# Attention with a routed feed-forward: the row transposes move into the accumulator's banks, value products follow their scores by 3 to 6 steps, and the first expert's rows are prepared earlier

## The chip, the core and the metric

The kernel runs on one core of a Trainium2 chip, in one launch. The core has a matrix engine (PE, whose weight loads are shown apart as PEld), a vector engine (DVE), a scalar engine (ACT), a general engine (POOL) and SyncE (SP), which here only issues transfers. DMA queues move data between memory and the on-chip buffers. Each engine runs its own instructions in order and waits on semaphores for the others. Matrix products land in accumulator banks; in this kernel a bank is a tile of 128 partitions by 512 fp32 numbers. The metric is the time of one execution in microseconds; lower is better.

## The reference

Attention over 8 batches, 12 heads, 448 positions and 64 columns a head, with soft-capped scores, and then a feed-forward whose expert is chosen per token, by a gate with a bias per modality:

```python
scores = scale * np.matmul(q, k.transpose(0, 1, 3, 2))
scores = cap * np.tanh(scores / cap)
scores = scores - np.max(scores, axis=-1, keepdims=True)
attn = np.exp(scores)
attn = attn / (np.sum(attn, axis=-1, keepdims=True) + 1e-09)
return np.matmul(attn, v).astype(np.float32)
...
logits = x @ w_gate + modality_bias[modality_id]
e_idx = np.argmax(logits, axis=1)
...
    h = np.maximum(x[mask] @ w1[e], 0.0)
    out[mask] = gate_w[mask, None] * (h @ w2[e])
```

Here `x` is the attention's result, 3584 tokens of 768 columns. There are 8 experts with 768 x 1024 and 1024 x 768 weights.

## The kernel before

**Attention.** Four heads make a group; there are 24 groups `d` (three to a batch), and each has 7 steps `s` of 64 keys. Step `n = 7d + s` is, in this order: the scores of 64 keys against all queries of four heads (`scores`, L445, into one of two `sc` tiles of two banks each), a tanh over them on ACT (L449), and after every second step one exp over both steps (L452). `weigh` multiplies the weights with the values (L467) into the accumulator `xT`, which is one tile of two banks, and follows the scores by `LAG` = 4 steps; its place is shifted around s = 4 and 5 (no value products at s = 4, two at s = 5). DVE adds the weights up over the steps (L473 and L475, `tot`) and copies the accumulator out after the seventh (L478, `kept`). `pin` keeps an instruction in the order in which the program was written, on its engine.

**Rows.** At s = 4 of group d four things follow the scores on PE. `logits(d - 2)` turns the sums and gate products of an earlier group (L496), and DVE takes reciprocals and scales them (L499, L505). `go_on` gives the pending routing its next piece (L240 and L242 on PE are its rank). `tokens(d - 2)` transposes the four heads' result into token rows (L520), which DVE scales (L527, one instruction) and a DMA stores to `xd` (L534). `sums(d - 1)` multiplies sums and gate weights (L485, L487), copied out at L489. The tile `tp` of `tokens` is taken from the pool of `sc` (tag "sc", two tiles in turn), so transposes and scores share four banks.

**Routing.** `start_route` after a batch's third group picks each token's expert in small DVE pieces and scatters token numbers and weights into a map in memory by four indirect DMAs (L266, tile `pay`, one buffer). `gate_bias` loads modality numbers and bias table and builds the bias with five DVE instructions (L195, L196, L203); the loads are issued on SP at the start of group 1.

**The way to the feed-forward.** The last batch's tokens are routed late, and work begins with one tile of 384 tokens of an expert that has as many among the first seven batches. SOON = 20 is the last group of the seventh batch. Its routing runs at (d, s) = (21, 6) and (22, 2), where `early_slot` also counts the tokens (L281 on PE) and DVE picks the expert (`emeta`, L301). At (22, 4) come the token rows of group 20, stored by SP, and the load of the map (`mt`, L677), which waits for the scatters. At (23, 1) POOL gathers the 384 rows (`xg`, L686, three indirect DMAs). The first expert's w1 comes in six blocks, each split into a high part (cast, L704) and the rest (L705): blocks 0, 1 and 2 on POOL at (22, 6) and (23, 1), block 3 on DVE at (23, 5), blocks 4 and 5 cast on ACT and subtracted on DVE after the loop. Then `move` transposes the gathered rows on PE (L722), split by ACT (L731) and DVE (L732), among the last value products.

**Feed-forward.** Slots of 384 tokens: `ffn1` (L749, L750, L753, tile `ph`, three buffers) and `ffn2` (L778). In the first slot the remaining sums, logits, routing and slot table of the last batch are put between the `ph` products. This part takes the time from about 375 us on.

**Start.** Six products of ones (`warm`, L160) run while the cap is loaded; the flag read follows, then four more, then the scores.

The line that shares the banks, and the two that set the lag:

```python
tp = ps_s.tile([128, 2, 512], F32, name="tp", tag="sc")
...
for m in range(n - LAG - (s == 5), n - LAG + (s != 4)):
    if m >= 0:
        weigh(m)
```

## Time and profile before

| | us |
|---|---|
| median of three runs (902.51 to 909.3) | 905.6 |
| the profiled execution | 906.49 |
| its span, from the first instruction to the last | 904.9 |
| first scores on PE start | 7.94 |
| last tanh of the attention starts | 357.15 |
| first product of the feed-forward starts | 375.04 |
| busy: PE, ACT, DVE, POOL | 850.4, 531.8, 515.4, 157.1 |

Busy time on PE is modelled at the ends of products, so a product's own duration overlaps the next; what PE needs for a piece of work is read from start to start. A row of a timeline gives the start, the duration, the engine, the line, what is written from what, and in brackets how long the engine was idle before and whom it waited for. PE counts each fp32 product as two instructions, so a step's four score products show as x8.

### The profile page before, as it was taken

Reading aid. Unit: us, or ns where it says so; the run is one execution under the profiler, and the core shown is the slowest. Engines: PE = TensorE matmul, PEld = TensorE weight load, DVE = VectorE, ACT = ScalarE, POOL = GpSimd, SP = SyncE. Lnnn points to the kernel's source line nnn. Section 1 sums busy time; section 2 is a strip of 40 time slices with the busy share of each in tenths; the row PEclk is TensorE's granted clock in tenths of the full one; section 3 lists DMA queues with packets and bytes.
Section 4 is the critical chain, followed back from the end, with each engine's and each line's share of the span. In section 5 each row is a group of like instructions: output and inputs, shape, how many; then the busy total and the mean of one; then the engine's idle time right before and its main releaser. Section 6 shows DMA issues by size and latency. Waiting matters only on the chain. (4 is left out here: it accounts for less than half of the span.)

```text
span 904.9 us, 15828 instructions
## 1 busy us (share of the span) xinstructions
PE 850.4 (94%) x6208; PEld 637.5 (70%) x6208; DVE 515.4 (57%) x867; ACT 531.8 (59%) x624; POOL 157.1 (17%) x161
## 2 busy tenths in 40 slices
PE   7799999999999998698999999999999999999996
PEld 2233334333343333598999999999999999989896
DVE  2568777778686877665443443444343344447861
ACT  6698898988989888315443442444433343436551
POOL 2000302031211214725202020120203011021000
PEclk9899999999999999699999999999999999999998
DMA  4235444363644456518735355464535446447650
GB/s 134 89 122 164 102 143 121 126 158 99 154 106 140 109 140 205 166 42 266 257 109 193 114 168 193 151 234 134 200 121 167 147 156 211 135 141 230 212 188 6
DMA packets 44284, 136.92 MB, mean 151 GB/s; under 512 B 8526, under 2 KB 9102, under 8 KB 44192
## 3 DMA queue, kind: packets, MB, share of 16 engines
q1 hardware_dynamic: 35008, 103.10, 36.6%
q0 software_dynamic: 9040, 32.64, 11.5%
q8 instruction: 52, 0.85, 0.4%
q14 instruction: 40, 0.33, 0.1%
q10 hardware_dynamic: 144, 0.00, 0.0%
HBM read 114.20 MB, written 22.69 MB: 151 GB/s over the span
## 5 line engine op out<-in xcount | busy, mean ns | idle before, releaser
L449 ACT ACTIVATE pt<-sc,isc 128x896 f32<-128x896 f32 x168 | 162.7, 996 | 46.7 <-PE sc L445 45.5
L753 PE MATMUL ph<-x,al 128*128 128x384 f32 (+2 forms) x528 | 168.2, 319 | 0.0
L778 PE MATMUL py<-bh,hh 128*128 128x384 f32 x464 | 158.5, 342 | 1.2 <-ACT hh L759 1.2
L778 PE MATMUL py<-bh,hl 128*128 128x384 f32 x464 | 155.8, 336 | 0.0
L778 PE MATMUL py<-bl,hh 128*128 128x384 f32 x464 | 155.3, 335 | 0.0
L467 PE MATMUL xT<-pt,va 64*64 64x448 f32 x1344 | 153.7, 542 | 0.0
L452 ACT ACTIVATE pt<-pt,cabs 128x1792 f32<-128x1792 f32 x84 | 150.3, 1789 | 2.7
L475 DVE TENSOR_TENSOR tot<-tot,pt 128x896 f32<-128x896 f32 x120 | 133.1, 1109 | 23.7 <-ACT pt L452 19.0
L749 PE MATMUL ph<-x,ah 128*128 128x384 f32 x384 | 130.3, 339 | 4.5 <-DVE x L732 4.4
L750 PE MATMUL ph<-x,ah 128*128 128x384 f32 x384 | 129.7, 338 | 0.0
L705 DVE TENSOR_TENSOR bl<-raw,bh 128x768 fp32r<-128x768 f32 x84 | 77.7, 955 | 50.0 <-ACT bh L704 49.9
L467 PEld LDWEIGHTS xT<-pt,va 64*64 64x64 f32 x1344 | 51.8, 135 | 76.4 <-issue 76.3
L704 ACT CAST bh<-raw 128x768 fp32r<-128x768 f32 x88 | 70.2, 839 | 57.0 <-DMA raw<-in_w_dram 52.7
L753 PEld LDWEIGHTS ph<-x,al 128*128 128x128 f32 x528 | 102.3, 194 | 0.0
L788 POOL DMA_INDIRECT out_dram<-ot,mt x29 | 32.0, 1105 | 385.8 <-ACT ot L783 308.4
L759 ACT ACTIVATE hh<-ph 128x384 fp32r<-128x384 f32 x64 | 30.6, 488 | 108.1 <-PE ph L753 105.2
L445 PE MATMUL sc<-kq 64*64 64x448 f32 x672 | 83.0, 569 | 9.8 <-ACT pt L449 9.0
L783 ACT ACTIVATE ot<-py,mt 128x384 f32<-128x384 f32 x58 | 33.7, 581 | 95.6 <-PE py L778 52.6
L778 PEld LDWEIGHTS py<-bh,hh 128*128 128x128 f32 x464 | 87.1, 188 | 1.6 <-ACT hh L759 1.5
L778 PEld LDWEIGHTS py<-bl,hh 128*128 128x128 f32 x464 | 87.2, 188 | 0.2 <-DVE bl L705 0.2
L778 PEld LDWEIGHTS py<-bh,hl 128*128 128x128 f32 x464 | 87.1, 188 | 0.1
L760 DVE SCALAR_TENSOR_TENSOR hl<-ph,hh 128x384 fp32r<-128x384 f32 x64 | 34.9, 555 | 91.7 <-ACT hh L759 91.5
(157 smaller groups left out, 1053.3 us busy)
## 6 DMA issues: line engine op xcount, KB each, us to landing
raw<-in_w_dram SPq DMA_DIRECT2D x88, 384.0 KB, 4.9
raw<-in_w_dram SPq DMA_DIRECT2D x64, 512.0 KB, 4.8
kq<-in_kq_dram SPq DMA_DIRECT2D x24, 448.0 KB, 5.0
va<-in_v_dram SPq DMA_DIRECT2D x24, 448.0 KB, 6.0
kx<-in_kq_dram SPq DMA_DIRECT2D x24, 448.0 KB, 4.4
xd<-xs POOLq DMA_DIRECT2D x23, 448.0 KB, 4.0
kq<-in_w_dram SPq DMA_DIRECT2D x2, 512.0 KB, 6.5
mapd<-pay,pos POOLq DMA_INDIRECT x32, 8.2
```

The costliest lines, as they stand in the source:

```text
L445: pin(pe.matmul(sc[i * KB : (i + 1) * KB, j, :S], kq[rows, s * KB : (s + 1) * KB], kq[rows, S:QK], start=True, stop=True,))
L449: pin(nc.scalar.activation(weights(n), sc[:, :, :S], AF.Tanh, scale=self.isc))
L452: pin(nc.scalar.activation(pt, pt, AF.Exp, scale=self.cabs))
L467: pin(pe.matmul(self.xT[j * D : (j + 1) * D, i, :S], vas[d][rows, o : o + D], pt[rows, j], start=s == 0, stop=s == STEPS - 1,))
L475: pin(V.tensor_tensor(tots[d], tots[d], pt, op=ALU.add))
L704: keep((cast.tensor_copy if cast else self.nc.scalar.copy)(hi, raw))
L705: keep((minus or self.nc.vector).tensor_tensor(lo, raw, hi, op=ALU.subtract))
L749: nc.tensor.matmul(ph[:, :w], hi[:, fs], self.x[:, k, 0, :w], start=first, stop=False)
L750: nc.tensor.matmul(ph[:, :w], hi[:, fs], self.x[:, k, 1, :w], start=False, stop=False)
L753: nc.tensor.matmul(ph[:, :w], lo[:, fs], self.x[:, k, 0, :w], start=False, stop=last)
L760: nc.vector.scalar_tensor_tensor(hl[:, f, :w], acc, 0.0, hh[:, f, :w], op0=ALU.max, op1=ALU.subtract)
L778: nc.tensor.matmul(py[:, :HALF], self.h[a][:, f, rows], self.w2s[f][c][:, cs], start=i == 0, stop=i == 3 * FC - 1,)
```

## The change

Value products get a table: `LAGS` gives for each step how many steps later it is weighed, 5, 5, 5, 5, 4, 4, 3 in even groups and 6, 5, 5, 5, 4, 4, 3 in odd ones, and `LAST` for the last group. With it no value products stand at s = 3 and 4, and the accumulator is copied out at s = 2 of the next group. The transposes of `tokens` take the accumulator's tile (tag "xT" of `ps_x`), at s = 4; the scaling is two DVE instructions, one for each bank. `sums` moves to s = 5, after that step's scores. `logits` is split: `turn` transposes and takes the reciprocals ahead of `tokens`, the scaling of the logits follows it. The additions leave `weigh` and run four steps behind the scores (`add`, `BEHIND`). The modality loads are issued at step 0 and used at (1, 3). Ahead of the first scores 18 products of ones run in one piece instead of six and four.

Near the end: the piece of routing and `early_slot` move from (22, 2) to (22, 1); the rows of group 20 from (22, 4) to (22, 2), into two banks of other pools and with their store ahead of the map's load on SP; the map's load to (22, 2); the gather from (23, 1) to (22, 4); all w1 loads to (22, 2), with blocks 4 and 5 in tiles of their own; the splits 0, 1, 2 and 3 to (22, 2), (22, 4), (22, 4) and (23, 4). Four `move`s instead of three stand ahead of the last two value products, in the banks of `sc`. The last group's remaining four additions and its copy come after all moves. `pay` has two buffers.

```diff
-LAG = 4
+LAGS = ((5, 5, 5, 5, 4, 4, 3), (6, 5, 5, 5, 4, 4, 3))
+LAST = (6, 5, 4, 4, 4, 4, 4)
+BEHIND = 4
...
+    def fetch_bias(self):
...
+        pay = pool.tile([CP, C, 2], F32, name="pay" if tok is not None else f"pay{b % 2}")
...
+            def add(n):
+
+                d, s = divmod(n, STEPS)
+                if s == 1:
+                    tots[d] = xp.tile([128, 2, S], F32, name="tot", bufs=2)
+                if s:
+                    pin(V.tensor_tensor(tots[d], pt_of(n - 1) if s == 1 else tots[d], pt_of(n), op=ALU.add))
...
-                if s == 1:
-                    tots[d] = xp.tile([128, 2, S], F32, name="tot", bufs=2)
-                    pin(V.tensor_tensor(tots[d], pt_of(n - 1), pt, op=ALU.add))
-                elif s:
-                    pin(V.tensor_tensor(tots[d], tots[d], pt, op=ALU.add))
-                if s == STEPS - 1:
-                    kept[d] = xp.tile([128, 2, S], F32, name="xT", bufs=3)
-                    pin(V.tensor_copy(kept[d], self.xT[:, :, :S]))
+
+            def keep(d):
+                kept[d] = xp.tile([128, 2, S], F32, name="xT", bufs=3)
...
-            def logits(d):
+            def turn(d):
...
+
+            def logits(d):
+
...
-                    tp = ps_s.tile([128, 2, 512], F32, name="tp", tag="sc")
+                    tp = ps_x.tile([128, 2, 512], F32, name="tp", tag="xT")
...
-                if not banks:
-                    src = tp[:CP].rearrange("p i (c j d) -> p i c j d", c=C, j=2)
-                    pin(V.tensor_tensor(dst, src, norm, op=ALU.mult))
...
+                for i in range(2):
+                    src = tps[i][:CP].rearrange("p (c j d) -> p c j d", c=C, j=2)
+                    pin(V.tensor_tensor(dst[:, i], src, norm[:, i], op=ALU.mult))
...
-                    raws[k] = self.load_raw(self.first_e, self.w1, k, FF, firsts[k - 4] if k >= 4 else None)
+                    spare = xp.tile([128, FF], F32, name="spare", bufs=2) if k >= 4 else None
+                    raws[k] = self.load_raw(self.first_e, self.w1, k, FF, spare)
...
-            self.warm(self.ps_r, 4)
+            END = STEPS * ND
+            due = [[] for _ in range(END + 1)]
+            for m in range(END):
+                d, s = divmod(m, STEPS)
+                due[min(m + (LAST if d == ND - 1 else LAGS[d % 2])[s], END)].append(m)
...
-                        self.gate_bias()
+                    if d == 0:
+                        self.fetch_bias()
...
                 scores(n)
-                if s == 6 or s == 1 and d != SOON + 2:
+                if n >= BEHIND:
+                    add(n - BEHIND)
+                if (d, s) == (1, 3):
...
-                if s == 4 and d:
-                    if d >= 2 and d - 2 != SOON:
+                if s == 4 and d >= 2:
+                    if d - 2 == SOON:
+                        self.gather(maps, known=NT - S)
+                    else:
+                        turn(d - 2)
+                        go_on()
+                        tokens(d - 2)
                         logits(d - 2)
-                    if d >= 2:
-                        go_on()
-                        tokens(d - 2, nc.sync if d - 2 == SOON else nc.gpsimd)
+                if s == 5 and d:
                     sums(d - 1)
-                    if d - 2 == SOON:
-                        maps = self.rows(meta, 0, early=True)
-                        load_w1((2, 3))
-                    elif d >= 2 and (d - 2) % NU == NU - 1:
+                    if d >= 2 and d - 2 != SOON and (d - 2) % NU == NU - 1:
                         start_route((d - 2) // NU)
-                for m in range(n - LAG - (s == 5), n - LAG + (s != 4)):
-                    if m >= 0:
-                        weigh(m)
+                for m in due[n]:
+                    weigh(m)
+                    if m % STEPS == STEPS - 1:
+                        keep(m // STEPS)
                 if (d, s) == (SOON + 1, 6):
+                    turn(SOON)
                     logits(SOON)
                     start_route(SOON // NU)
                     go_on()
                     go_on()
-                if (d, s) == (SOON + 2, 2):
+                if (d, s) == (SOON + 2, 1):
                     go_on()
                     meta = self.early_slot(self.cpool, self.ps_r)
                     self.first_e = self.expert(meta, 0)
                     load_w1((0, 1))
-                if (d, s) == (SOON + 2, 6):
+                if (d, s) == (SOON + 2, 2):
+                    tokens(SOON, nc.sync, (self.ps_r, "small"), (ps_g, "glog"))
+                    maps = self.rows(meta, 0, early=True)
+                    load_w1((2, 3, 4, 5))
                     split(0, nc.gpsimd, nc.gpsimd)
-                if (d, s) == (SOON + 3, 1):
-                    self.gather(maps, known=NT - S)
+                if (d, s) == (SOON + 2, 4):
                     split(1, nc.gpsimd, nc.gpsimd)
                     split(2, nc.gpsimd, nc.gpsimd)
-                if (d, s) == (SOON + 3, 5):
+                if (d, s) == (SOON + 3, 4):
                     split(3, V, V)
 
...
-            def move(k):
-                self.transpose(k, *((self.ps_r, "small") if k % 3 == 2 else (ps_s, "sc")), pin=True)
-
-            n = STEPS * ND
-            weigh(n - 4)
-            weigh(n - 3)
+            def move(k, pt):
+                self.transpose(k, None, None, pin=True, pt=pt)
+
+            for n in due[END][:2]:
+                weigh(n)
             split(4, None, V)
-            for k in range(3):
-                move(k)
-            weigh(n - 2)
-            weigh(n - 1)
+            pair = [ps_s.tile([128, 2, 512], F32, name="ptr", tag="sc") for _ in range(2)]
+            for k in range(4):
+                move(k, pair[k // 2][:, k % 2])
+            for n in due[END][2:]:
+                weigh(n)
             split(5, None, V)
-            for k in range(3, KC):
-                move(k)
+            move(4, self.ps_r.tile([128, 512], F32, name="ptr", tag="small"))
+            move(5, ps_g.tile([128, 512], F32, name="ptr", tag="glog"))
+            for n in range(END - BEHIND, END):
+                add(n)
...
+                turn(ND - 2)
...
+                turn(ND - 1)
...
-                    self.warm(ps_w, 6)
+                    self.warm(ps_w, 18)
```

On PE, the stretch of an even group around the transposes. `sc` are scores, `lt` the turned sums and logits, `tp` the token rows, `glog` the products of sums and gate, `xT` the value products. Before:

```order
L445 MATMUL sc<-kx 64x448 [waits Activation_49]
L445 MATMUL sc<-kx 64x448 x3
L496 MATMUL lt<-ident,gl 112x128 [waits DVE_49]
L496 MATMUL lt<-ident,gl 112x128 x3
L520 MATMUL tp<-ident,xT 112x128 [waits Activation_49]
L520 MATMUL tp<-ident,xT 112x128 x7
L485 MATMUL glog<-tot,pick 32x448 [waits DVE_49]
L485 MATMUL glog<-tot,pick 32x448
L487 MATMUL glog<-xT,wgt 32x448 [waits DVE_49]
L487 MATMUL glog<-xT,wgt 32x448
L445 MATMUL sc<-kx 64x448 [waits Activation_49]
L445 MATMUL sc<-kx 64x448 x3
```

And in the changed kernel, where these rows stand at the same place in another such group:

```order
L506 MATMUL lt<-ident,gl 112x128 [waits DVE_49]
L506 MATMUL lt<-ident,gl 112x128 x3
L534 MATMUL tp<-ident,xT 112x128 [waits DVE_49]
L534 MATMUL tp<-ident,xT 112x128 x7
L451 MATMUL sc<-kx 64x448 [waits Activation_49]
L451 MATMUL sc<-kx 64x448 x3
L495 MATMUL glog<-tot,pick 32x448 [waits DVE_49]
L495 MATMUL glog<-tot,pick 32x448
L497 MATMUL glog<-xT,wgt 32x448 x2
L451 MATMUL sc<-kx 64x448 [waits Activation_49]
L451 MATMUL sc<-kx 64x448 x3
L481 MATMUL xT<-pt,va 64x448 [waits DMAHW1_49,DVE_49,PE_49]
```

The transposes no longer wait for ACT but for DVE's copy of the accumulator, the next scores stand straight behind them, and the wait for DVE's reading of `tp` has moved from a later score to the next group's first value product.

On DVE at the start, groups 0 and 1 (`modi` and `mbt` are the modality numbers and the bias table). Before, the bias stands behind the second addition:

```order
L473 TENSOR_TENSOR tot<-pt 128x896 [waits Activation_49]
L475 TENSOR_TENSOR tot<-tot,pt 128x896 [waits DVE_49,Activation_49]
L195 TENSOR_SCALAR sel<-modi 112x32 [waits DMAHW3_49]
L196 TENSOR_TENSOR bias<-sel,mbt 112x256 [waits DMAHW4_49,DVE_49]
L195 TENSOR_SCALAR sel<-modi 112x32 [waits DVE_49]
```

Now it stands behind the first group's copy of the accumulator and its last addition:

```order
L469 TENSOR_TENSOR tot<-tot,pt 128x896 [waits DVE_49]
L488 COPY xT<-xT 128x896 [waits PE_49]
L469 TENSOR_TENSOR tot<-tot,pt 128x896 [waits DVE_49,Activation_49]
L201 TENSOR_SCALAR sel<-modi 112x32 [waits DMAHW0_49]
L202 TENSOR_TENSOR bias<-sel,mbt 112x256 [waits DMAHW1_49,DVE_49]
L201 TENSOR_SCALAR sel<-modi 112x32 [waits DVE_49]
```

All six of the first group's additions have moved ahead of the wait for `modi`.

On DVE behind the last scores (`al` is the rest of a w1 block, `x` the rest of the gathered rows, `hl` the first result of the feed-forward). Before:

```order
L705 TENSOR_TENSOR al_157<-kq,ah_156 128x1024 [waits DMAHW4_49,DMAHW0_49,Activation_49]
L732 TENSOR_TENSOR x<-ptr,x 128x384 [waits Activation_49] x3
L475 TENSOR_TENSOR tot<-tot,pt 128x896 [waits DVE_49] x2
L478 COPY xT<-xT 128x896 [waits PE_49]
L705 TENSOR_TENSOR al_159<-kq,ah_158 128x1024 [waits DMAHW5_49,DMAHW1_49,Activation_49]
L732 TENSOR_TENSOR x<-ptr,x 128x384 [waits Activation_49] x3
```

Now:

```order
L732 TENSOR_TENSOR al_169<-spare,ah_168 128x1024 [waits DMAHW4_49,Activation_49]
L760 TENSOR_TENSOR x<-ptr,x 128x384 [waits Activation_49] x4
L732 TENSOR_TENSOR al_171<-spare,ah_170 128x1024 [waits DMAHW5_49,Activation_49]
L760 TENSOR_TENSOR x<-ptr,x 128x384 [waits Activation_49] x2
L469 TENSOR_TENSOR tot<-tot,pt 128x896 [waits DVE_49] x4
L488 COPY xT<-xT 128x896
```

Four additions and the copy have moved behind everything that the feed-forward's first products need; two additions and the copy stood among it.

## Rows read from the trace of the kernel before

**Rows 1.** The page's first part: busy time of the matrix engine (products, then weight loads) and its share of the span.

```profile
PE 850.4 (94%) x6208; PEld 637.5 (70%) x6208; DVE 515.4 (57%) x867; ACT 531.8 (59%) x624; POOL 157.1 (17%) x161
```

**Rows 2.** Busy time of each engine in stretches (start:end, length, then each engine's busy us and instructions, the granted clock, the DMA share, GB/s): the feed-forward's first 5 us (of the instructions of L749 alone), 100 us of the feed-forward, and a period of two groups in mid-attention.

```profile
375.00:380.00 5.00, 2.77 (x6) 1.94 (x6) 0.50 0.68 235
...
600.00:700.00 100.00, 100.00 (x594) 99.64 (x594) 41.51 (x54) 40.58 (x65) 13.86 (x12) 1.00 0.49 163
...
67.94:96.38 28.44, 27.09 (x270) 11.13 (x266) 22.52 (x44) 25.55 (x22) 1.41 (x3) 1.00 0.41 131
```

**Rows 3.** Timeline of ACT: the tanh of step 12 (39.50), one period of two groups from step 26 on (67.94 to 82.28, not all its rows), and the tanh of step 152 (324.25).

```profile
39.50 1.01 ACT L449 ACTIVATE pt<-sc,isc 128x896 f32<-128x896 f32 x1 [7.15 <-PE sc L445]
...
67.94 1.01 ACT L449 ACTIVATE pt<-sc,isc 128x896 f32<-128x896 f32 x1 [0.29 <-PE sc L445]
70.22 1.01 ACT L449 ACTIVATE pt<-sc,isc 128x896 f32<-128x896 f32 x1 [1.27 <-PE sc L445]
...
72.96 1.89 ACT L449 ACTIVATE pt<-sc,isc 128x896 f32<-128x896 f32 x2
...
76.57 1.89 ACT L449 ACTIVATE pt<-sc,isc 128x896 f32<-128x896 f32 x2
...
82.28 1.01 ACT L449 ACTIVATE pt<-sc,isc 128x896 f32<-128x896 f32 x1 [1.10 <-PE sc L445]
...
324.25 1.01 ACT L449 ACTIVATE pt<-sc,isc 128x896 f32<-128x896 f32 x1 [0.29 <-PE sc L445]
```

**Rows 4.** Timeline of PE in the same period, around two groups' transposes.

```profile
69.20 0.93 PE L445 MATMUL sc<-kx 64*64 64x448 f32 x8
69.95 0.93 PE L467 MATMUL xT<-pt,va 64*64 64x448 f32 x8
...
78.53 0.65 PE L496 MATMUL lt<-ident,gl 128*112 128x128 f32 x4
79.01 1.04 PE L520 MATMUL tp<-ident,xT 128*112 128x128 f32 x8
79.98 0.57 PE L485 MATMUL glog<-tot,pick 128*32 128x448 f32 x2
...
91.37 0.93 PE L445 MATMUL sc<-kx 64*64 64x448 f32 x8
92.23 0.65 PE L496 MATMUL lt<-ident,gl 128*112 128x128 f32 x4
...
94.44 0.57 PE L485 MATMUL glog<-tot,pick 128*32 128x448 f32 x2
...
95.33 0.98 PE L445 MATMUL sc<-kx 64*64 64x448 f32 x8
```

**Rows 5.** Timeline at the start: PE's first products of ones and first scores, ACT's first two tanhs, the modality load on SP and DVE's wait for it.

```profile
1.56 2.10 PE L160 MATMUL idle<-ones 112*128 112x384 bf16 x6 [1.56 <-DVE ones L130]
...
7.94 5.38 PE L445 MATMUL sc<-kq 64*64 64x448 f32 x32
...
9.78 1.01 ACT L449 ACTIVATE pt<-sc,isc 128x896 f32<-128x896 f32 x1 [6.92 <-PE sc L445]
...
11.27 1.01 ACT L449 ACTIVATE pt<-sc,isc 128x896 f32<-128x896 f32 x1 [0.49 <-PE sc L445]
...
22.51 0.42 SPq L89 DMA_DIRECT2D modi<-in_mod_dram  x1
...
28.80 0.18 DVE L195 TENSOR_SCALAR sel<-modi 112x32 f32<-112x32 int32 x1 [9.96 <-DMA modi<-in_mod_dram]
```

**Rows 6.** Timeline of all engines from the turning of group 20 (327.12) to the feed-forward's first product: additions, the first scatter, map load, gather, last tanh, moves and last value products.

```profile
327.12 0.65 PE L496 MATMUL lt<-ident,gl 128*112 128x128 f32 x4
...
331.54 3.34 DVE L475 TENSOR_TENSOR tot<-tot,pt 128x896 f32<-128x896 f32 x3
...
336.46 0.97 POOL L266 DMA_INDIRECT mapd<-pay,pos  x1 [11.80 <-DVE esc L298]
...
349.56 0.33 SPq L677 DMA_DIRECT2D mt<-mapd  x1
...
356.72 1.14 POOL L686 DMA_INDIRECT xg<-xd,mt  x1 [3.47 <-DMA xd<-xs]
...
357.15 1.01 ACT L449 ACTIVATE pt<-sc,isc 128x896 f32<-128x896 f32 x1 [1.25 <-PE sc L445]
...
365.21 1.13 PE L722 MATMUL ptr<-identr,xg 128*128 128x128 f32 x7 [1.86 <-DMA xg<-xd,mt]
...
366.27 3.27 PE L467 MATMUL xT<-pt,va 64*64 64x448 f32 x16
...
375.04 0.66 PE L749 MATMUL ph<-x,ah 128*128 128x384 f32 x1 [4.36 <-DVE x L732]
```

**Rows 7.** Timeline of DVE and POOL in the same stretch: subtractions and additions, alone and beside the other engine.

```profile
357.78 1.23 DVE L705 TENSOR_TENSOR al<-raw,ah 128x1024 fp32r<-128x1024 f32 x1
...
362.25 2.06 DVE L705 TENSOR_TENSOR al<-kq,ah 128x1024 fp32r<-128x1024 f32 x1
...
367.53 4.29 DVE L475 TENSOR_TENSOR tot<-tot,pt 128x896 f32<-128x896 f32 x2
...
362.09 1.13 POOL L704 CAST ah<-raw 128x1024 fp32r<-128x1024 f32 x1
...
372.81 8.18 POOL L705 TENSOR_TENSOR bl<-raw,bh 128x768 fp32r<-128x768 f32 x4 [1.29 <-ACT bh L704]
```

More of the change, by code (lines that the diff above doesn't have):

```diff
@@ L178, in empty_map @@
         self.load(self.mapd[E * RG :].rearrange("(p r) t -> p (r t)", p=128), src[:, : 2 * TW])
[L180 to L188 removed]
+    def fetch_bias(self):
+        cpool = self.cpool
+        self.modi = cpool.tile([CP, B, C, 2], I32, name="modi")
+        self.load(
+            self.modi.rearrange("p b c t -> p b (c t)"),
+            self.mod.bitcast(I32).rearrange("(b p x) -> p b x", b=B, p=CP),
+        )
+        self.mbt = cpool.tile([CP, NM, E], F32, name="mbt")
+        self.load(self.mbt, self.mb.unsqueeze(0).to_broadcast([CP, NM, E]))
+    def gate_bias(self):
+        nc, cpool, modi, mbt, pin = self.nc, self.cpool, self.modi, self.mbt, self.pin
         self.bias = cpool.tile([CP, B * C, E], F32, name="bias")
@@ L714, in load_w2, with transpose @@
             self.split_w(raw, self.w2s[k], pin=bool(raws), minus=minus)
-    def transpose(self, k, pool, tag, busy=False, n=TW, pin=False):
+    def transpose(self, k, pool, tag, busy=False, n=TW, pin=False, pt=None):
         nc = self.nc
         keep = self.pin if pin else (lambda inst: inst)
-        pt = pool.tile([128, 512], F32, name="ptr", tag=tag)
+        if pt is None:
+            pt = pool.tile([128, 512], F32, name="ptr", tag=tag)
         w = n * 128
@@ L862, in general @@
             self.empty_map()
+            self.fetch_bias()
             self.gate_bias()
```

43 lines of the change are left out of this document (17 added, 26 removed).

## Prediction

> **What bounds the kernel now.** I read the page's engine shares first: PE is busy for 850.4 us [rows 1], 94% of the span. From about 380 us on it runs the feed-forward's products with no gap worth naming (100 us hold 594 products, 0.168 us each, at full clock [rows 2]), and the change touches nothing there but the first slot. What can be won lies ahead of it. So next I read ACT's timeline over one period of two groups, 14 steps. From the tanh of step 12 to that of step 152 are 284.75 us, ten periods of 28.44 to 28.6 [rows 3]. ACT alone needs less: two steps, tanh to tanh, take 3.61 us where nothing waits (72.96 to 76.57 [rows 3]), 25.3 for 14, and the window of one period has ACT busy for 25.55 of 28.44 [rows 2]. It idles for 0.29, 1.27 and 1.10 us, each time for scores from PE [rows 3].
>
> PE's busy share there, 27.09 of 28.44 [rows 2], overstates what it needs, since ends are modelled. From start to start, one step's scores or value products take 0.75 us (69.20 to 69.95 [rows 4]), 21.0 for the 28 of a period. Each group adds 0.11 where scores are followed by transposes (91.37 to 92.23 is 0.86), 0.48 for the turning (78.53 to 79.01), 0.97 for the token rows (79.01 to 79.98) and 0.89 for sums and gate (94.44 to 95.33) [rows 4]: 2.45. So PE needs 21.0 + 4.9 = 25.9 of 28.44. Neither engine is full: they wait for each other, at the place where the transposes take one of the two score tiles. The next scores then cannot start before the tanh just ahead of them is done.
>
> **Start.** The first scores come at 7.94 and the first two tanhs at 9.78 and 11.27 [rows 5], 1.49 apart where ACT itself needs about 1.0: PE is at half its later pace. From there ACT is full. If 18 products in one piece bring the clock up before the scores, tanh 0 comes 1.02 after the scores, as in mid-attention (69.20 in [rows 4], 70.22 in [rows 3]), and tanh 1 one later: -1.3. But six of them took 2.10 [rows 5]; 18 at that pace end at about 7.9, and the flag read comes after, so scores could start at 8.5 still slow: +0.6. I take -0.8.
>
> **Modality table.** DVE waited 9.96 us for `modi`, issued at 22.51 and there 6.3 later [rows 5]. The additions behind it held back the weights' buffers, and ACT idled for 7.15 ahead of step 12 [rows 3]. Issued at step 0 instead of 7, some 12 us sooner at 1.8 us a step, and used after the first group's additions, that wait is gone: -7.2. Its cover is the time from step 0 to step 10 of ACT's work, some 18 us; had it none, the old price would stand.
>
> **Mid-attention.** The transposes now wait for DVE's copy of the accumulator, taken two steps earlier, and scores keep both their tiles. PE's need becomes 25.9 + 0.22 for one more change between scores and 128-row products in each group + about 0.3 for the rank products of a routing, which only every third group has: 26.4, above ACT's 25.3. The lower bound is thus 26.4, the upper one the old 28.44. I take 26.7, near the lower, because in the new order PE meets no wait that the old trace shows to be late: the copy of the accumulator has the scores of s = 3 and 4 and the turning to end in (2.1 us), and DVE, busy for 22.5 us in a period with routing [rows 2], has room in 26.7 even with 0.1 more for each split instruction. Ten periods: 284.75 - 267 = -17.8.
>
> **Steps 152 to 167.** They took 32.9 us (324.25 to 357.15, [rows 3, 6]), with a wait around the early routing. 15 steps at 26.7 for 14 are 28.6; 0.3 more since PE runs ahead of ACT at (22, 3) to (22, 5): -4.0. POOL's splits beside DVE's additions could cost 2.
>
> **To the first feed-forward product.** Call t the start of the last tanh. Before, t = 357.15, and `ph` began 17.9 later [rows 6]. What ends last is the gather: it began at 356.72, having waited for the store of rows, and its third tile reached PE at 365.21, 8.5 later [rows 6]. In the change the store is ahead of the map's load on SP, so the map comes last. From the turning of group 20 (327.12) to the first scatter (336.46) were 9.34 us with three additions of 1.1 in between [rows 6]; now two stand there: 8.2. From the scatter to the map's load 13.1 (349.56), which SP spent waiting for the scatters to land. For the map itself I take 2 (bounds 0.3, its issue, and 7.2, when the gather began). Then 8.5 for the gather: the rows are there 31.8 after the turning. The turning stands 2.4 after its step's scores (0.80 and two times 0.75 and a change), the last tanh 14 steps later: 26.7 + 0.3 + 1.0 - 2.4 = 25.6 after the turning. So the rows arrive at t + 6.2, not much sooner than before (t + 8.1), because the attention that covers them got shorter. Behind them on PE: ten transposes of 0.16 (seven in 1.13), two steps of value products (1.5 at full clock, 3.27 as they were at half [rows 6]; I take 2.3), six transposes: 4.9. `ph` starts at t + 11.1: -6.8, bounds -9 and -3.
>
> **Clock.** From 375 to 380 the granted clock was 0.50, the lower level (1.2 GHz), after PE had waited twice, for the gather and for `x` [rows 2, 6]; so half of those 5 us, 2.5, was lost. PE now waits once: its products after t end by about t + 3.5, the rows come at t + 6.2. I take -1.0, bounds 0 and -2.5.
>
> **What is late next.** The last group's four additions and its copy now come after all `x`. PE reaches the products that need them after 40 `ph` products, 6.7 us after it began [rows 2]. DVE comes to the additions about 1.5 after `ph` began, and POOL then subtracts four w2 blocks of 2.05 (8.18 [rows 7]). Alone, additions (4.4) and copy (1.1) end at 7.0: a wait of 0.3. But two additions beside POOL took 4.29 instead of 2.2, and a subtraction that starts 0.2 after a POOL cast 2.06 instead of 1.23 [rows 7]; if each addition but the first waits for a POOL subtraction, DVE ends at 1.5 + 4.4 + 3 x 2.05 + 1.1 = 13.1, and PE waits for 6.4. I take 5, nearer the rows' collisions.
>
> The row of 4.29 alone leaves open whether the second addition waited for POOL or for its own input. The Trainium skill, "SBUF — State Buffer", section "Who interferes with whom", says that a DVE instruction with two SBUF inputs and a GpSimd instruction that reads SBUF exclude each other for a whole instruction. By that rule the term is 6.4 and the sum 875; by the reading that denies it, 0.3 and 869. The row of 2.06, with no input late, agrees with the rule. It speaks against putting additions beside POOL's subtractions.
>
> **Sum.** On the profiled execution (906.49; its span 904.9, so 1.6 lie outside; the median of the runs is 905.6): -0.8 - 7.2 - 17.8 - 4.0 - 6.8 - 1.0 + 5.0 = -32.6, and 906.5 - 32.6 = 874. The feed-forward behind the first slot is taken as unchanged: the count of `ph` products ahead of the slot table's count (90) is the same in both orders, and the second slot's gather hangs on that.
>
> **Rivals.**
> Bubbles stay: if the periods are PE's real need, as its 94% suggests [rows 1], the mid-attention term is 0 and the last 15 steps still take 30.5 (-2.4): 893. Against it: PE's starts leave 2.5 us a period unused [rows 4], about the sum of ACT's three idle times. Chance 0.12, with half of it a time between 884 and 893.
> The accumulator becomes the stall: the next group's first value product now waits for DVE to have read the transposes, and PE, in order, holds everything behind it. Between the transposes and that product PE has the next scores and the sums, 1.7 us; DVE needs some 1.3 for 1024 columns (an estimate from 1.1 for an addition of 896) and up to 0.9 of routing pieces ahead of it. Without the gains of mid-attention and the last steps the sum is 895.7, so it is slower than before once each of 22 groups waits 0.5 more than it loses today, about 1.5 us; at 1.6 it is 908. DVE would then need 3.2, half as much again as the 2.2 that stand in its queue. Chance 0.03.
> The transition gives nothing: rows no sooner than t + 11, because scatters land later beside five weight loads: 881. Chance 0.08.
> Better: no collision on DVE and PE at its need: 864. Chance 0.07.
> The forecast, 866 to 882: 0.70.
>
> **Range.** 864 to 890 leaves out the slower rival, the upper half of the bubbles and the tail below. About 1% is what a measurement of this kernel can tell. Over 1% faster (below 896.5) are the forecast, the better case, the poor transition and most of the bubbles: 0.93; within 1%: 0.04; slower: 0.03.
>
> **What would show it.** Tanhs of steps 26 and 40 26.4 to 27 us apart, PE without gaps around the transposes, and no ACT idle over 1 us a period: mid-attention. Step 12's tanh near 31.5: start and table. `ph` about 11 us after the last tanh, its first transposes waiting for the gather: the transition. Four additions of over 2 us each beside POOL's subtractions and PE waiting for them before the last `glog`: the DVE term. The prediction fails if first value products wait for DVE in each group, or if the period stays above 28.

## The result, and the profile after

The changed kernel takes 870.3 us (median of four runs, 868.4 to 872.4), the kernel before 905.6: a ratio of 0.961 (95% interval 0.957 to 0.965). The profiled execution has 869.5 us and a span of 867.9 in place of 904.9, 37.0 less. Cut at five instructions that both traces show, the 37.0 lie here (t is the start of the last tanh; a row with x2 holds two tanhs, the second one starting 0.99 before the row ends):

| stretch | before | after | difference | predicted |
|---|---|---|---|---|
| start to tanh of step 12 | 39.50 | 30.27 | -9.2 | -0.8 - 7.2 |
| tanh 12 to tanh 152 | 284.75 | 263.87 | -20.9 | -17.8 |
| tanh 152 to t (step 167) | 32.90 | 30.15 | -2.8 | -4.0 |
| t to the first `ph` product | 17.89 | 18.84 | +0.9 | -6.8 |
| first `ph` product to the end | 529.86 | 524.77 | -5.1 | -1.0 + 5.0 |

Busy time of PE, ACT, DVE and POOL in the page's first part, against [rows 1]:

```profile
PE 835.6 (96%) x6216; PEld 635.6 (73%) x6216; DVE 515.4 (59%) x889; ACT 529.3 (61%) x624; POOL 153.2 (18%) x161
```

The timeline of ACT after the change, for [rows 3]: tanh 12, the tanh of step 152 (first of its row), ACT's two longest waits behind it, and the last tanh (second of its row).

```profile
30.27 1.89 ACT L455 ACTIVATE pt<-sc,isc 128x896 f32<-128x896 f32 x2
...
294.14 1.88 ACT L455 ACTIVATE pt<-sc,isc 128x896 f32<-128x896 f32 x2
...
299.26 0.23 ACT L227 ACTIVATE ex<-L 112x32 f32<-112x32 f32 x1 [1.41 <-DVE L L225]
...
305.52 1.01 ACT L455 ACTIVATE pt<-sc,isc 128x896 f32<-128x896 f32 x1 [1.52 <-PE sc L451]
...
323.39 1.89 ACT L455 ACTIVATE pt<-sc,isc 128x896 f32<-128x896 f32 x2
```

The windows that answer to [rows 2]: a period of mid-attention, the wait between attention and feed-forward, the feed-forward's first 6.9 us, 100 us of it.

```profile
38.81:65.21 26.40, 26.40 (x268) 11.05 (x264) 19.37 (x27) 25.38 (x22) 1.62 (x2) 1.00 0.45 141
...
324.35:343.13 18.78, 9.37 (x74) 4.27 (x67) 14.69 (x11) 6.47 (x10) 10.48 (x6) 0.73 0.60 220
343.13:350.00 6.87, 6.87 (x42) 6.86 (x41) 6.29 (x7) 1.74 (x4) 0.02 (x1) 1.00 0.00 0
...
600.00:700.00 100.00, 100.00 (x594) 99.55 (x592) 42.94 (x55) 41.74 (x67) 13.87 (x12) 1.00 0.51 169
```

This period is 26.40 us (26.39 on the mean of ten) and PE is busy for all of it; ACT, busy for 25.4, has what idle time there is. The feed-forward runs as before. Around a group's transposes PE goes from turning to rows to the next scores without a gap (for [rows 4]):

```profile
65.82 0.65 PE L506 MATMUL lt<-ident,gl 128*112 128x128 f32 x4
66.31 1.04 PE L534 MATMUL tp<-ident,xT 128*112 128x128 f32 x8
67.27 0.98 PE L451 MATMUL sc<-kq 64*64 64x448 f32 x8
68.18 0.57 PE L495 MATMUL glog<-tot,pick 128*32 128x448 f32 x2
...
69.07 0.98 PE L481 MATMUL xT<-pt,va 64*64 64x448 f32 x8
```

The first value product at 69.07, which waits for DVE to have read the rows, has no idle time behind it either. At the start (for [rows 5]) the products of ones run on until the scores, the scores start at once at full pace, two steps in 1.82, and DVE's first use of `modi` shows no wait:

```profile
1.56 5.94 PE L162 MATMUL idle<-ones 112*128 112x384 bf16 x18 [1.56 <-DVE ones L132]
...
7.43 1.82 PE L451 MATMUL sc<-kq 64*64 64x448 f32 x16
8.57 1.90 ACT L455 ACTIVATE pt<-sc,isc 128x896 f32<-128x896 f32 x2 [5.70 <-DVE meta L371]
8.97 0.43 SPq L91 DMA_DIRECT2D modi<-in_mod_dram  x1
...
27.28 0.18 DVE L201 TENSOR_SCALAR sel<-modi 112x32 f32<-112x32 int32 x1
```

Where the prediction failed is the way to the feed-forward. The timeline of all engines there, for [rows 6] and [rows 7]:

```profile
296.33 0.65 PE L506 MATMUL lt<-ident,gl 128*112 128x128 f32 x4
...
304.53 0.99 POOL L272 DMA_INDIRECT mapd<-pay,pos  x1 [8.07 <-DVE esc L304]
...
319.13 0.35 SPq L704 DMA_DIRECT2D mt<-mapd  x1
...
321.63 1.08 POOL L713 DMA_INDIRECT xg<-xd,mt  x1 [4.66 <-DMA mt<-mapd]
...
325.00 1.96 DVE L731 CAST ah<-raw 128x1024 fp32r<-128x1024 f32 x1 [1.97 <-DMA raw<-in_w_dram]
...
325.36 1.04 POOL L731 CAST ah<-raw 128x1024 fp32r<-128x1024 f32 x1
...
326.49 2.71 POOL L732 TENSOR_TENSOR al<-raw,ah 128x1024 fp32r<-128x1024 f32 x1
...
326.99 3.28 DVE L732 TENSOR_TENSOR al<-raw,ah 128x1024 fp32r<-128x1024 f32 x1
...
329.14 2.03 POOL L731 CAST ah<-raw 128x1024 fp32r<-128x1024 f32 x1
...
330.20 1.92 DVE L469 TENSOR_TENSOR tot<-pt 128x896 f32<-128x896 f32 x1
331.25 3.11 POOL L732 TENSOR_TENSOR al<-raw,ah 128x1024 fp32r<-128x1024 f32 x1
...
332.57 2.73 DVE L469 TENSOR_TENSOR tot<-tot,pt 128x896 f32<-128x896 f32 x1
...
333.15 0.37 PE L750 MATMUL ptr<-identr,xg 128*128 128x128 f32 x1 [1.37 <-DMA xg<-xd,mt]
...
336.37 0.54 DVE L760 TENSOR_TENSOR x<-ptr,x 128x384 fp32r<-128x384 f32 x1
...
336.96 1.00 PE L750 MATMUL ptr<-identr,xg 128*128 128x128 f32 x6 [3.44 <-DVE x L760]
...
339.21 0.62 PE L750 MATMUL ptr<-identr,xg 128*128 128x128 f32 x3 [1.25 <-DVE x L760]
...
343.13 0.41 PE L777 MATMUL ph<-x,ah 128*128 128x384 f32 x1
...
344.53 4.46 DVE L469 TENSOR_TENSOR tot<-tot,pt 128x896 f32<-128x896 f32 x4
...
349.07 3.04 ACT L731 CAST bh<-raw 128x768 fp32r<-128x768 f32 x4 [5.13 <-DVE tot L469]
...
349.98 7.22 POOL L732 TENSOR_TENSOR bl<-raw,bh 128x768 fp32r<-128x768 f32 x4 [14.98 <-ACT bh L731]
...
372.25 0.34 PE L806 MATMUL py<-bh,hh 128*128 128x384 f32 x1
```

The last row is the first `py`, with which the first half of the first slot ends. In the kernel before:

```profile
407.13 0.34 PE L778 MATMUL py<-bh,hh 128*128 128x384 f32 x1
```

Read the stretch up to `ph` in three parts. The last rows come to PE at 333.15, t + 8.9, 11.5 after the gather began (8.5 before). From 326.5 to 335.3 DVE's and POOL's instructions take turns: DVE's subtraction ends 1.07 after POOL's (329.20 and 330.27), its addition 0.95 after POOL's cast (331.17 and 332.12), the next 0.94 after POOL's subtraction (334.36 and 335.30), each thus a little less than its own length (1.23, 1.08 and 1.08 where nothing is beside it) after the other engine. And PE then waits twice for DVE's `x`, 3.44 and 1.25 us.

### The profile page after: what moved, and what is told of

Same layout as the page of the kernel before. It is cut to its first block, busy times and chain, and to the rows that moved or that the text cites. A ratio compares the mean times of both kernels' runs of the same rounds, so it can differ in the third digit from the quotient of the medians.

```text
span 867.9 us, 15885 instructions
## 1 busy us (share of the span) xinstructions
PE 835.6 (96%) x6216; PEld 635.6 (73%) x6216; DVE 515.4 (59%) x889; ACT 529.3 (61%) x624; POOL 153.2 (18%) x161
## 5 line engine op out<-in xcount | busy, mean ns | idle before, releaser
L481 PE MATMUL xT<-pt,va 64*64 64x448 f32 x1344 | 147.2, 542 | 0.0
L732 DVE TENSOR_TENSOR al<-raw,ah 128x1024 fp32r<-128x1024 f32 x61 | 74.7, 1256 | 22.1 <-ACT ah L731 22.0
L760 DVE TENSOR_TENSOR x<-ptr,x 128x384 fp32r<-128x384 f32 (+2 forms) x66 | 32.8, 517 | 92.0 <-ACT x L759 92.0
```

The source lines that it names most:

```text
L481: pin(pe.matmul(self.xT[j * D : (j + 1) * D, i, :S], vas[d][rows, o : o + D], pt[rows, j], start=s == 0, stop=s == STEPS - 1,))
L732: keep((minus or self.nc.vector).tensor_tensor(lo, raw, hi, op=ALU.subtract))
L760: keep(nc.vector.tensor_tensor(lo, pt[:, :w], hi, op=ALU.subtract))
```

## The experiments

The experiments ran on four chips: E1 to E4 on one, E5 to E8, E9 to E11 and E12 on one each. The kernel before had a median of 901.9, 908.0, 903.7 and 906.7 us on them, so each ratio is against the kernel before on the same chip, with its interval. The stretches are those of the table above, from each kernel's profiled execution.

| kernel | median | ratio to before | tanh 12 at | 12 to 152 | 152 to t | t to `ph` | `ph` to end |
|---|---|---|---|---|---|---|---|
| changed, first run | 870.3 | 0.961 (0.957-0.965) | 30.27 | 263.87 | 30.15 | 18.84 | 524.8 |
| E1 rows in `sc` | 893.6 | 0.990 (0.988-0.992) | 30.31 | 284.55 | 31.00 | 19.52 | 528.5 |
| E2 before, rows in `xT` | 896.3 | 0.992 (0.990-0.994) | 37.57 | 277.23 | 36.27 | 16.18 | 528.4 |
| E3 before, table first | 896.8 | 0.994 (0.992-0.996) | 31.99 | 283.47 | 32.90 | 17.83 | 526.8 |
| E4 six and four | 874.7 | 0.968 (0.965-0.971) | 32.02 | 263.88 | 30.14 | 20.30 | 526.2 |
| E5 own tiles | 873.2 | 0.961 (0.959-0.963) | 30.08 | 267.67 | 29.63 | 17.26 | 527.3 |
| E6 no splits on POOL | 873.2 | 0.960 (0.956-0.963) | 30.42 | 267.67 | 30.15 | 16.80 | 527.9 |
| E7 weights before map | 873.9 | 0.962 (0.959-0.964) | 29.27 | 267.66 | 31.27 | 17.84 | 526.9 |
| E8 additions first | 879.3 | 0.969 (0.966-0.971) | 30.43 | 267.77 | 29.74 | 24.69 | 523.8 |
| E9 one lag | 886.4 | 0.980 (0.979-0.982) | 30.37 | 277.78 | 31.31 | 19.71 | 527.3 |
| E10 changed again | 873.2 | 0.965 (0.963-0.967) | 29.79 | 263.87 | 30.16 | 20.26 | 527.5 |
| E11 all ahead of rows | 866.2 | 0.958 (0.956-0.960) | 29.32 | 263.87 | 30.15 | 13.33 | 525.4 |
| E12 sums at 4 | 873.4 | 0.962 (0.958-0.966) | 29.93 | 265.09 | 32.88 | 17.53 | 526.6 |

E10 is the changed kernel itself: between its two profiles, t to `ph` differs by 1.4 and the last column by 2.7. Differences of that size in the last two columns say nothing. E5 to E8, on one chip, share 267.7 where others have 263.9, though their edits lie behind that stretch: between 65 and 290 us ACT waits 9.7 us for scores in E5 and 6.3 in the changed kernel. Why is open, and there the column compares within the four. The medians of E5 to E8 lie 3 us or more above the times that their expectations name, and this 3.8 is part of it; what each edit does is read from its own stretch.

**E1: the transposes' tile alone put back.**

```diff
-                    tp = ps_x.tile([128, 2, 512], F32, name="tp", tag="xT")
+                    tp = ps_s.tile([128, 2, 512], F32, name="tp", tag="sc")
```

> The changed kernel with one thing put back: the row transposes take a tile from the pool of the scores again (lags, order, additions and all else stay as changed). Theory (shared banks made the scores wait for the tanh just ahead of them): a period of two groups goes from 26.4 back to 27.5 to 28.5 us, ten and a half of them are 12 to 22 us, so 882 to 892, with ACT idle around each group's transposes. Rival (the longer lags and the additions four steps behind brought the gain, the bank did not matter): the period stays at 26.4 to 26.6 and the time at 869 to 873.

Mid-attention is back at 284.55, as before the change: without the tile, lags, additions and order bring nothing there. The median of 893.6 is just above the 882 to 892 expected. The waits of PE and of ACT between 65 and 290 us (total, times, longest):

```profile
PE sc L451 <- ACT pt L455: 12.8, 8, 1.6
...
ACT pt L455 <- PE sc L451: 20.1, 32, 1.1
```

In the changed kernel PE has no such wait in that stretch, and ACT this one:

```profile
ACT pt L455 <- PE sc L451: 6.3, 9, 0.8
```

**E2: the tile alone, in the kernel before**, the same line the other way round.

> The kernel before with one thing of the change: the row transposes take the accumulator's tile; the lag of 4 stays, so two steps of value products stand right behind the sums and wait for DVE to have read the rows. Theory (bank alone): the scores keep their two tiles, the period falls from 28.45 to 26.6 to 27, so 886 to 892. Rival (the bank pays only with the new lags, since PE in order now stands at the first value product until DVE has scaled the rows): the period stays at 27.8 to 28.5 or more, 900 to 910.

277.23 is between theory and rival, 27.7 a period: the tile alone brings 7.5 of the 20.9, and 3.4 of it goes again in the last 15 steps (36.27). So the prediction's reason, shared banks, is needed (E1) and is not enough.

**E9: the lags alone put back.**

```diff
-LAGS = ((5, 5, 5, 5, 4, 4, 3), (6, 5, 5, 5, 4, 4, 3))
+LAGS = ((5, 4, 4, 4, 4, 4, 4), (5, 4, 4, 4, 4, 4, 4))
```

> The changed kernel with the kernel before's placing of value products: a lag of 4 throughout, and of 5 for the first step of a group, so that value products stand at s = 3 again, two steps of them at s = 5, and the accumulator is copied out at s = 3. Rows stay in the accumulator's banks, additions four behind, sums at s = 5. Theory (both are needed: the tile lets scores run ahead of ACT, the table gives PE the room to do so before the transposes): a period of 27 to 27.7 us, 6 to 13 us over ten periods, so 5 to 12 more than the changed kernel of the same call. Rival (tile, order of sums and additions suffice, the exact lags do not matter): 26.4 to 26.8 a period, within 3 of the changed kernel.

277.78, a period of 27.8, just past the range expected, and the whole is 13 us slower than E10 beside it. That is close to E2's 277.23: the tile is worth 7 to 7.5 without the new lags, and the lags 13.9 with the tile. ACT's and PE's waits are between those of E1 and of the changed kernel:

```profile
PE sc L451 <- ACT pt L455: 4.1, 12, 0.4
...
ACT pt L455 <- PE sc L451: 15.5, 21, 1.2
```

**E12: sums put back to s = 4.**

```diff
-                if s == 5 and d:
+                if s == 4 and d:
                     sums(d - 1)
+                if s == 5 and d:
```

> The changed kernel with one thing of the order put back: sums and gate products stand at s = 4, right behind the transposes, as in the kernel before; tile, lags and additions stay as changed. Theory (what counts is how much PE does between two steps' scores, since ACT has work for two tiles at most): between the scores of s = 4 and s = 5 PE then has 2.4 us of other work in place of 1.5, more than ACT's 1.8 for a step, and a period goes from 26.4 to 27 to 27.8, 6 to 14 us over ten periods. Rival (with the accumulator's tile and the new lags PE has run far enough ahead there to take it): 26.4 to 26.6 a period, a time within 2 of the changed kernel's.

The rival held: 265.09, 26.5 a period, though PE does as much between two scores as the theory feared. That the lags give PE a lead over ACT, and that this lead covers 2.4 us as well as 1.5, is a reading and not shown: from the scores of s = 4 to their tanh are 2.9 to 3.0 us on the mean in even groups in the changed kernel and in E12, and 2.6 in E9, but in odd groups 1.8 to 1.9 in all three. Which part of the lags does it (no value products at s = 3 and 4, or the accumulator copied out a step sooner) was not tried. In the last 15 steps E12 loses 2.7, where ACT waits 2.66 once for scores.

**E3: the modality table loaded first, in the kernel before.**

```diff
                     fetch(d + 1)
+                    if d == 0:
+                        self.fetch_bias()
                     if d == 1:
                         self.gate_bias()
```

> The kernel before with one thing of the change: modality numbers and bias table are loaded at step 0, and used at the start of group 1 as before. Theory (DVE waited for a load that was issued late, and ACT behind it): ACT's 7.15 us ahead of step 12 are gone, tanh 12 comes at 32.3 in place of 39.5, and the time is 898 to 899. Rival (the later place of use is needed too, since the bias still stands ahead of the first group's additions, or the loads at the start delay keys and values): at most half of it, 902 or more.

Tanh 12 at 31.99, 7.51 sooner: the theory. The later place of use is not needed.

**E4: the products of ones as before.**

```diff
-                    self.warm(ps_w, 18)
+                    self.warm(ps_w, 6)
...
+            self.warm(self.ps_r, 4)
             fetch(0)
```

> The changed kernel with one thing put back: six products of ones ahead of the flag read and four behind it, in place of 18 ahead. Theory (18 products bring the clock up before the first scores): tanh 1's exp comes at 12.3 in place of 10.51, and all behind it, ACT being full from there, so +1.8 and 871 to 873. Rival (the prediction's size): +0.8. Other rival: PE gains the lost time back behind the start, where it has slack until step 12, and the time does not change by more than 0.5.

Tanh 12 comes 1.75 later, and 12 to 152 is the same to 0.01, so none of it is regained. With E3's 7.5 this makes the 9.2 of the first stretch. What its ratio shows beyond that is E10's spread.

**E6: blocks 1 and 2 of w1 not split by POOL.**

```diff
-                if (d, s) == (SOON + 2, 4):
-                    split(1, nc.gpsimd, nc.gpsimd)
-                    split(2, nc.gpsimd, nc.gpsimd)
...
-            split(4, None, V)
+            for k in (1, 2, 4):
+                split(k, None, V)
```

> The changed kernel with blocks 1 and 2 of w1 split by ACT (casts) and DVE (subtractions) behind the loop, not by POOL. DVE gets two subtractions of 1.23 more. Theory (from 326.5 to 335.3 us DVE's and POOL's instructions with SBUF operands alternate, each waiting for the other): DVE's block, additions and the like shrink to 0.7, 1.2 and 1.1 us each, its first x comes 2.4 us sooner though it does more, and the first feed-forward product at t + 16 to 17 in place of t + 18.8; 864 to 865 where the changed kernel has 867. Rival (DVE's instructions are long for a reason of their own, a late load or the bank they read): DVE ends 2.5 later, t + 21, 869 to 870.

The same DVE instructions (cast, subtraction, two additions) in E6, where POOL splits nothing beside them:

```profile
328.55 0.69 DVE L729 CAST ah<-raw 128x1024 fp32r<-128x1024 f32 x1 [2.12 <-DMA raw<-in_w_dram]
329.27 1.23 DVE L730 TENSOR_TENSOR al<-raw,ah 128x1024 fp32r<-128x1024 f32 x1
...
330.42 1.08 DVE L469 TENSOR_TENSOR tot<-pt 128x896 f32<-128x896 f32 x1
...
331.95 1.08 DVE L469 TENSOR_TENSOR tot<-tot,pt 128x896 f32<-128x896 f32 x1
```

0.69, 1.23, 1.08, 1.08 where the changed kernel has 1.96, 3.28, 1.92, 2.73: the lengths were waits for POOL. `ph` comes at t + 16.8, as expected. The whole time does not show it: 873.2, as in E5 beside it.

**E5: four tiles for the first four blocks**, in place of two.

```diff
-            pair = [ps_s.tile([128, 2, 512], F32, name="ptr", tag="sc") for _ in range(2)]
-            for k in range(4):
-                move(k, pair[k // 2][:, k % 2])
+            own = ((ps_s, "sc"), (ps_s, "sc"), (self.ps_r, "small"), (ps_g, "glog"), (ps_s, "sc"), (ps_s, "sc"))
...
+            for k in range(4):
+                move(k, bank(k))
```

> The changed kernel with one thing put back: the transposes of the gathered rows each get a tile of their own (two of the scores' pool, the small one, the gate's; the last two take the first two again), in place of two blocks to a tile. Theory (PE's waits of 3.44 and 1.25 us for DVE's x come from the sharing, since the second block of a tile waits until DVE has read the first): blocks 0 to 3 are moved without a wait once the rows are there, and the first feed-forward product comes 3 to 5 us sooner, at t + 14 to 16 (t the last tanh) in place of t + 18.8; 862 to 864 where the changed kernel has 867. Rival (DVE itself is late, behind POOL, and x would be late from any tile): t + 18 or more, a time within 1 of the changed kernel's.

PE's two waits are gone (ten transposes in 1.51 us), but `ph` is at t + 17.3: DVE, still behind POOL, writes its first `x` at t + 13.1, and PE waits at the end instead. That is between theory and rival, nearer the rival: sharing and POOL each hide the other.

**E7: w1 blocks 2 to 5 ahead of the map on SP.**

```diff
-                    maps = self.rows(meta, 0, early=True)
                     load_w1((2, 3, 4, 5))
+                    maps = self.rows(meta, 0, early=True)
```

> The changed kernel with SP's order turned round: w1 blocks 2 to 5 are loaded ahead of the map's load, which waits for the scatters, not behind it. Theory (the three gathers land 8.4 us after their start, where they took 5.0 before, because 2 MB of weights were issued 2 us ahead of them): they land 5 to 6 after their start, rows at t + 6 in place of t + 8.8. What that is worth is bounded by DVE, which is busy beside POOL until 335.3: 0 to -3 us. Rival (the loads then run beside the scatters, which land later, and the map and the gather with them): map load 2 to 4 us later, rows no sooner, 866 to 870.

The map's load, the first gather, and PE's first transposes, each waiting for one gather (started at 329.91, 331.29 and 332.62):

```profile
323.90 0.34 SPq L704 DMA_DIRECT2D mt<-mapd  x1
...
329.91 1.08 POOL L713 DMA_INDIRECT xg<-xd,mt  x1 [10.31 <-DMA mt<-mapd]
...
333.99 0.25 PE L750 MATMUL ptr<-identr,xg 128*128 128x128 f32 x1 [2.19 <-DMA xg<-xd,mt]
...
336.09 0.37 PE L750 MATMUL ptr<-identr,xg 128*128 128x128 f32 x1 [1.85 <-DMA xg<-xd,mt]
...
337.75 0.37 PE L750 MATMUL ptr<-identr,xg 128*128 128x128 f32 x1 [1.29 <-DMA xg<-xd,mt]
```

The theory was right on the gathers and the rival on the rows. The gathers arrive 4.1, 4.8 and 5.1 after their start where the changed kernel's landed after 8.4. But the map's load comes 17.1 after the first scatter (14.6), and the map 6.0 after its load (2.5). The rows are there at t + 9.6, no sooner than at t + 8.9. The Trainium skill, "DMA: Bandwidth & Descriptors", section "Issuing engines are not separate DMA queues", says that transfers of all issuing engines interleave on the same 16 DMA engines. The trace agrees: moving the weights moves the delay from POOL's gather to SP's map and POOL's scatters.

**E8: the last four additions ahead of the moves.**

```diff
+            for n in range(END - BEHIND, END):
+                add(n)
             split(4, None, V)
...
-            for n in range(END - BEHIND, END):
-                add(n)
             keep(ND - 1)
```

> The changed kernel with the last four additions put ahead of the transposes of the gathered rows and of the last blocks, on DVE (the copy of the accumulator stays last). Theory (DVE is full from 325 to 336 and stands ahead of every x): 4.4 us of additions more ahead of the first x, more where they meet POOL, so the first feed-forward product comes at t + 22 to 25, 870 to 873 where the changed kernel has 867. Rival (they fill time in which DVE waits anyway): t + 19, 866 to 868.

`ph` at t + 24.7, the largest effect of E5 to E8, and 879.3 where the other three have 873 to 874: DVE's work ahead of `x` sets the end of this stretch, and the change was right to put the additions last.

**E11: what E5 and E6 point to, together, and all that needs no rows ahead of the rows.**

```diff
-            for n in due[END][:2]:
+            for n in due[END]:
                 weigh(n)
-            split(4, None, V)
...
+            for k in (1, 2, 4, 5):
+                split(k, None, V)
+            own = ((ps_s, "sc"), (ps_s, "sc"), (self.ps_r, "small"), (ps_g, "glog"), (ps_s, "sc"), (ps_s, "sc"))
+            for k in range(KC):
+                pool, tag = own[k]
+                move(k, pool.tile([128, 512], F32, name="ptr", tag=tag))
```

Block 0 moves to DVE at (22, 6).

> The changed kernel with four things put where the runs show room: no block of w1 is split by POOL (block 0 on DVE at the end of group 22, blocks 1, 2, 4, 5 cast by ACT and subtracted by DVE), all value products and all splits stand ahead of the transposes of the gathered rows, each of which gets a tile that it shares with none in use. Theory (PE's last wait is then the gather's alone): rows at t + 8.5 to 9, then 2.4 us of transposes, the first feed-forward product at t + 11 to 12, 7 sooner than in the changed kernel; four additions beside block 0 take 4.4 in place of 7.3 and the last 15 steps 1 less; 8 less in all. Rival (the low clock level, which now runs out while PE waits, then falls into the first products): 3 to 5 of it is given back behind the first product, 3 to 5 less in all. Second rival (the four subtractions on DVE are late themselves): t + 14 or more, 3 less or nothing.

```profile
332.90 2.53 PE L745 MATMUL ptr<-identr,xg 128*128 128x128 f32 x16 [1.51 <-DMA xg<-xd,mt]
333.73 2.88 DVE L755 TENSOR_TENSOR x<-ptr,x 128x384 fp32r<-128x384 f32 x6 [0.16 <-ACT x L754]
...
336.67 0.69 PE L772 MATMUL ph<-x,ah 128*128 128x384 f32 x1 [1.23 <-DVE x L755]
```

`ph` at t + 13.3, 6.9 sooner than in E10 beside it; the median is 866.2 against 873.2, and the intervals are apart. This is faster than both kernels. Of what was expected, 1.2 goes to a wait for the last `x`, and the rows come at t + 9.6, not 9. What each of E11's parts gives was not tried, apart from E5 and E6. The last 15 steps did not get shorter (30.15), though the additions beside block 0 now take 1.1 each: that part of the theory was wrong. Of the low clock level, E11 has more in the first products than the changed kernel, as the windows from the first product on show for E11 (0.73, against 1.00 above):

```profile
336.67:343.00 6.33, 6.33 (x27) 6.33 (x28) 5.22 (x5) 1.93 (x3) 1.01 (x1) 0.73 0.00 0
```

The first half of the first slot takes 31.0 us where E10 has 29.3, so 1.7 of the 6.9 is given back there. It did not eat the gain, in the profiles or in the medians.

## Why the prediction was right in the sum, and where its steps were not

The sum was -32.6 and the profile has -37.0; two terms were wrong by more than a few us and nearly cancelled (the transition 7.7 too good, DVE behind `ph` 5.0 too bad), and mid-attention, clock and start were each taken 1 to 3 too small. That the sum is closer than its steps is luck in that part.

- **Start, -0.8, and table, -7.2**: measured -1.75 (E4) and -7.5 (E3). The mechanism was right; the start was bounded at -1.3 because the scores were thought to begin at 7.94 and began at 7.43.
- **Mid-attention, -17.8**: -20.9. The lower bound, PE's need of 26.4 a period worked out from starts, was the time itself; 26.7 was too careful. (With it and no collision on DVE, the terms of the "better" rival add up to 866, not 864.) The cause named, shared banks, gives only 7.5 alone (E2). That the new lags are the other half (E9) stood in the prediction only as "PE meets no wait".
- **Steps 152 to 167, -4.0**: -2.8. ACT stands for 1.41 us ahead of 299.26 for a DVE piece of the early routing, where it stood for 0.70 before (330.06), and for 1.52 ahead of 305.52 for scores, behind PE's value products and the transposes of group 20's rows. The sum had neither wait; this is read, not tried. The cost named there, POOL's split beside additions, is real (four additions took 7.26) and moved no end (E11).
- **To the first product, -6.8**: +0.9, the step that failed. What read "the rows arrive at t + 6.2" came out at t + 8.9. From the turning (296.33) to the rows were 36.8 us and not 31.8: the gather took 11.5 for 8.5, scatters and map 2.0 more; 2.4 of this is hidden, because t itself came that much later after the turning. The 8.5 was from before, where each of the three gathers landed 4.9 to 5.2 after its own start; the last block of weights was issued 2.5 us ahead of the first (354.22 and 356.72). Here four blocks were issued in the 2 us ahead of it, and E7, without them there, is back at 4.1 to 5.1. And what stands behind them on PE, 4.9 to `ph` at t + 11.1, was 10.0, the larger part of the 7.7. It left DVE out, which was still splitting and adding beside POOL, so that `x` came 3.2 after the rows, and it left out PE's two waits for `x` at the shared tiles. The collision that the prediction put behind `ph` happened ahead of it. Without both, and with the value products ahead of the rows, E11 has t + 13.3.
- **Clock, -1.0**: the first half of the first slot, from the first `ph` to the first `py`, takes 29.1 us (343.13 to 372.25) where it took 32.1 (375.04 to 407.13), so -3.0. The forecast was that PE would wait once. It waited for the gather and twice for `x`, but the low level (granted clock 0.50, 1.2 GHz) stood from 331.9 to 342.2 and ended ahead of the first product. In the kernel before it came a second time in PE's last wait, 4.36 us for `x`, and stood from 373.7 to 380.5, which is the 0.50 of [rows 2]. The other profiles agree: with a granted clock of 0.94 to 1.00 over the 7 us from the first `ph` this half takes 29.1 to 29.6 us (the changed kernel, E1, E4, E6 to E10, E12), with 0.74 to 0.76 it takes 31.0 to 31.3 (E3, E5, E11), with 0.61 it takes 32.1 (before, E2).
- **DVE late behind `ph`, +5.0**: nothing. The four additions start 1.4 after `ph`, as forecast, and take 4.46, 1.1 each. POOL's w2 subtractions could not meet them: ACT's casts ahead of them waited 5.13 us for these additions (349.07), and POOL began at 349.98. The Trainium skill, "SBUF — State Buffer", section "Who interferes with whom", gives such a pair an exclusive lock. The trace agrees where the two meet, between 326 and 335, and E6 shows it by the lengths without POOL. The rule was right and the pair was not there.
- The remaining 2.1 behind the first slot's first half are within what E10 differs from the first run, 2.7.

Of the rivals, "bubbles stay" did not occur; E1 shows it, in the kernel without the tile. "The accumulator becomes the stall" did not occur: PE has no wait in mid-attention. "The transition gives nothing" came true mostly for other reasons than the one given (late scatters are 1.5 of it, the map's load 14.6 after the first scatter and not 13.1), and was paid back by the clock and by the collision that had moved.

## What to carry to other kernels

When two engines wait for each other, a buffer less shared may pay in full only with an order that goes with it (here 7.5 us alone and 20.9 with the new lags): try tile and order together, and read the goal from starts, not from busy shares. Cost a stretch in front of a fixed end by engine: a term that follows one chain (here the gather) must be held against what every other engine still has to do there. A transfer's time from one stretch does not hold for another in which megabytes were issued just ahead of it.

## What the hardware showed that was not expected

A DVE cast with one input in SBUF also took its turn with POOL: 1.96 us beside a POOL cast and 0.69 alone; POOL's own cast took 2.03 behind a DVE subtraction and 1.04 otherwise. The Trainium skill, "SBUF — State Buffer", section "Who interferes with whom", says so of casts in a 2-port mode; the trace agrees if these casts ran in one, which it does not show. Three gathers of 128 rows reached PE 8.5 to 8.8 us after their start with 2 MB of weights issued in the 2 us ahead of the first, and 4.1 to 5.1 after it in E7, where these were issued 16 us or more ahead. PE's low clock level (1.2 GHz) came with its long wait for rows and `x`, and how much of it fell behind that wait differed between two runs of one kernel, with granted clocks of 0.73 and 0.67 over the wait and 1.00 and 0.97 in the first products.
